# An output product with standing weights: six of eight chunk pairs turned, their sums transposed in 32x32 blocks behind the next pair

## The chip, the cores and the metric

The kernel runs on one core of a Trainium2 chip. The metric is the device time of one execution in microseconds (us). Before the change it is 1220.3 us, the median of three runs (1218.64 to 1220.49).

## The reference

What is computed, in NumPy, cut to what matters (4608 tokens of 512 features go in the middle part, all in float32):

```
a  = softmax(scale * x @ state.T);   xread = a @ state
a2 = softmax(scale * state @ x.T);   sread = a2 @ x
x  = concatenate([xread, sread], axis=2)        # (8, 8, 544, 64)
x  = x.transpose(0, 2, 1, 3).reshape(4352, 512)
h  = maximum(x @ w_in, 0)                       # 512 -> 2048
y  = h * h @ w_out                              # 2048 -> 512
h  = (y @ w1) * (y @ w2) @ w3                   # 512 -> 1024 -> 1024
out = h @ w_out2                                # (4352, 512)
```

The change concerns the last two lines, and there the product with `w3 @ w_out2`, which the kernel forms once as one matrix.

## The kernel before

The tokens are cut in eight chunks (one per batch) of 512 read tokens; the 256 state tokens of all batches are a ninth, small chunk. After the attention and the first feed-forward network, whose result `y` lies in DRAM, about 711 us into the span, the second network begins. It goes over the chunks in **two sweeps** (s=0 and 1, one for each half of the 1024 hidden features), each over four **pairs** of chunks, `turns = [(3,4), (5,6), (7,2), (0,1)]` forward and then backward. A pair of chunks is taken together because both feature products and output products are done by a fast matrix scheme for 2x2 blocks with seven block products instead of eight; the sums and differences of blocks that it needs are made on VectorE (DVE). Every float32 operand is split in a high and a low part (`split`: a cast on ScalarE, ACT, then a subtraction on DVE, L81 and L82), and each block product runs three passes (HI*HI, LO*HI, HI*LO).

A pair consists of four `quad` calls (L941, m = 0 to 3), seven products of six matmuls with 512 columns each (L945), and then an **out stage**, `out_pair` (L1071). In a quad, `kept` copies a bank from PSUM on ACT (L953, tiles `s0` to `s3`), `plus` adds another bank on DVE (L957), the two multiplications at L975 and L981 give `q1` and `q0`, and `to_z` (L901) makes from them the blocks B11, T1 and so on, that the out stage reads (tiles `z`, slots `c1` to `c6`). What is not needed at once is split later, by `late_z` (L923) inside the out stage.

`out_pair` runs seven products A11*B11, S1*T1, S4*B22, A12*B21, S2*T2, S3*T3 and A22*T4 (L1090). In each, a 128x128 block of **tokens stands** in PE and 256 columns of **weights move**: 24 matmuls per product. `keep` (L1111) copies a bank to SBUF on ACT, `put` (L1123) adds the other bank on DVE and stores the sum of output block "11", "12", "21" or "22" (two tiles each): in the first sweep by a plain DMA on the SP queue, in the second by an accumulating DMA on the POOL queue (L1136). Pair (3,4), the first of sweep 0 and the last of sweep 1, is the exception: its sums wait in a DRAM scratch (`oscr`), and in its last stage (`ends`) they are fetched and added before the only store. The tiles of the blocks are named by `AT`: block "11" lies in the slots `s0` and `s1`, which the next quad's `kept` uses too.

`load_turn` (L1059) replaces one of the four weight slots in the course of the stage (with the combinations for S4, then for S3), on the SP queue. `jobs` are pieces of the next pair's preparation (`make_pair`, splits of `yraw` into `yq`), put between the products. The order of the instructions on an engine follows from the written order and from a scheduler that fills in; `issue_after` keeps a piece behind a named instruction. Each engine works through its own list in order: an instruction that waits holds up what stands behind it.

Of the kernel before, what the change touches and what calls it, by code (L numbers as in the profile page):

```python
# [20 lines left out]
def kernel(  # L21
# [17 lines left out]
    nc = tc.nc  # L39
# [255 lines left out]
    def att_steps(b):  # L295
# [5 lines left out]
        def xpose(k):  # L301
            ps = bank_m("ps_x") if b else bank_y(k, "ps_x")
            for j in range(J):
                h0 = 2 * (k % 2)
                nc.tensor.transpose(
                    ps[:, j * P:(j + 1) * P],
                    X[b, k // 2][:, j, h0:h0 + 2, :].rearrange("p h d -> p (h d)"), ident,
                )
            t = att.tile([P, 512], F32, tag="xT", bufs=4, name="xT")
            xT[b, k] = t  # L310
            if b == 0 and k == HG - 1:
                return nc.vector.tensor_copy(t, ps)
            return nc.scalar.copy(t, ps)

        def scores():
            pss = [bank_m("ps_s") for _ in range(G)]
# [71 lines left out]
        def a2_T(r):  # L388
            ps = bank_m("ps_a2")
            e = v["a2", r]  # L390
            for j in range(J):
                nc.tensor.transpose(ps[:, j * P:(j + 1) * P], e[:, j * P:(j + 1) * P], ident)
            nc.scalar.copy(e, ps)

        def sread():
# [502 lines left out]
    def minus(t, a, b):  # L898
        return nc.vector.tensor_tensor(out=t, in0=a, in1=b, op=ALU.subtract)  # L899

    def to_z(m, q0, q1):  # L901

        idx = m // 2
        if m % 2 == 0:
            z_split(1 + idx, "B11", idx, q0)
            minus(q0, q1, q0)
            left["T1", idx], left["B12", idx] = q0, q1
            return z_split(3 + idx, "T1", idx, q0)
# [12 lines left out]
        return last  # L921
# [16 lines left out]
            z_split(6, "T4", 0, left.pop(("T4", 0)))  # L938
            z_split(2, "T4", 1, left.pop(("T4", 1)))

    def quad(c0, c1, m):  # L941
        def product(ps, w, v, first=True, last=True):
            for kt in range(2):
                for k, (wi, vi) in enumerate(PASSES):
                    nc.tensor.matmul(  # L945
                        ps, W[w, kt][:, wi, m * P:(m + 1) * P], Y[v, kt][:, vi, :],
                        start=(first and kt == 0 and k == 0), stop=(last and kt == 1 and k == 2),
                        skip_group_check=True,
                    )

        def kept(i, ps):
            t = bp.tile([P, 512], F32, tag=f"s{i}", bufs=1 + (i == 0), name=f"s{i}")
            left["copy"] = nc.scalar.copy(t, ps)  # L953
            return t

        def plus(t, ps):
            nc.vector.tensor_tensor(out=t, in0=ps, in1=t, op=ALU.add)  # L957
# [7 lines left out]
        plus(p1, E)  # L965
# [3 lines left out]
        plus(u2, D)  # L969
        product(C, "A22", "T4")  # L970
        product(A, "S3", "T3", first=False)
        u3 = kept(3, A)
        plus(p5, A)
        q1 = bp.tile([P, 512], F32, tag="qd" if m % 2 else "qb", bufs=1 if m % 2 else 2, name="q1")
        nc.vector.tensor_tensor(out=q1, in0=u2, in1=p5, op=ALU.mult)  # L975
        plus(u3, C)
# [4 lines left out]
        nc.vector.tensor_tensor(out=q0, in0=p1, in1=u3, op=ALU.mult)  # L981
        return to_z(m, q0, q1)

    def load9(pool, tag):
        ts = []
# [81 lines left out]
    def place(tag, name):  # L1067
        pool = pa if tag in ("yo", "r") else bp
        return pool.tile([P, 512], F32, tag=tag, bufs=2 if tag in TWO else 1, name=name)

    def out_pair(c0, c1, s, jobs, last, first, more):  # L1071
        ends = s == 1 and not more
        jobs, gate = list(jobs), left["copy"]
# [49 lines left out]
        def put(block, ts, ps, tp0=0):  # L1123
            c, i = where(block)
            for tp, t in enumerate(ts, tp0):
                nc.vector.tensor_tensor(out=t, in0=ps[tp - tp0], in1=t, op=ALU.add)  # L1126
                if s == 0 and first:
                    nc.sync.dma_start(scr(c, i, tp), t)
                    continue
                rows_t = "(p j) e -> p j e" if c < BLK else "(j p) e -> p j e"  # L1130
# [43 lines left out]
            load_turn(s, 1)  # L1174
        if ends:
            bC = [bank_y((2 + t) % 4, "oc") for t in range(4)]
            rows_t = "(p j) e -> p j e" if c0 < BLK else "(j p) e -> p j e"
# [38 lines left out]
    bp = ctx.enter_context(tc.tile_pool(name="bp", bufs=1, reuse_waits="tile"))  # L1216

    turns = [(3, 4), (5, 6), (7, 2), (0, 1)]
    raw9 = load9(bp, "s0")
    raw = load_pair(*turns[0])  # L1220
    make9(raw9)
# [4 lines left out]
    for s, todo in enumerate((turns, turns[::-1])):  # L1226
        if s == 1:
            for t in range(NT9 // P):
                load_o9(t)
        for m in range(QM):  # L1230
            ab9(m)
        for t in range(NT9 // P):
            out9(t, s)
        load_sums(s)
        load_turn(s, 1)
        for i, (c0, c1) in enumerate(todo):
            for m in range(QM):
                last = quad(c0, c1, m)
# [12 lines left out]
            out_pair(c0, c1, s, jobs, last, i == 0, more)  # L1251
# [33 lines left out]
```

## Time and profile before

| | |
|---|---|
| runs | 1218.64, 1220.3, 1220.49 us |
| profiled execution | 1219.03 us, span 1217.3 us |
| granted clock | 0.999 |
| busy in the span: PE / PE weight loads / DVE / ACT / POOL | 1201.4 / 999.6 / 869.4 / 662.2 / 109.4 us |
| a pair of the second sweep | 58.27 us: four quads of 9.5 us and an out stage of 20.2 us |

The profile is one execution, 1.7 us longer than its span. The chain that ended last is followed backward from the end; PE makes up most of it, which means that a stretch of time is as long as PE's work in it, unless PE waits. Busy time of another engine matters where PE, or a store at the end, waits for it.

### The profile page before, as it was taken

Reading aid. Unit: us, or ns where it says so; the run is one execution under the profiler, and the core shown is the slowest. Engines: PE = TensorE matmul, PEld = TensorE weight load, DVE = VectorE, ACT = ScalarE, POOL = GpSimd, SP = SyncE. Lnnn points to the kernel's source line nnn. Section 1 sums busy time; section 2 is a strip of 40 time slices with the busy share of each in tenths; the row PEclk is TensorE's granted clock in tenths of the full one; section 3 lists DMA queues with packets and bytes.
Section 4 is the critical chain, followed back from the end, with each engine's and each line's share of the span. In section 5 each row is a group of like instructions: output and inputs, shape, how many; then the busy total and the mean of one; then the engine's idle time right before and its main releaser. Section 6 shows DMA issues by size and latency. Waiting matters only on the chain.

```text
span 1217.3 us, 18891 instructions
## 1 busy us (share of the span) xinstructions
PE 1201.4 (99%) x7174; PEld 999.6 (82%) x7174; DVE 869.4 (71%) x1594; ACT 662.2 (54%) x1220; POOL 109.4 (9%) x163
## 2 busy tenths in 40 slices
PE   7999999999999999999999999999999999999998
PEld 5677777777778777778899888989898989898988
DVE  6968877677586766742435875878696957877877
ACT  6877466555464655654656653546363635453542
POOL 0000001322421121100000000000000000211110
PEclk9999999999999999999999999999999999999999
DMA  9445664835446397630413642223232540716244
GB/s 260 138 140 173 159 184 145 185 113 130 129 127 156 106 184 155 154 53 35 121 53 113 222 156 98 81 93 104 70 104 70 191 138 20 155 30 144 49 74 138
DMA packets 147922, 150.66 MB, mean 124 GB/s; under 512 B 81016, under 2 KB 107128, under 8 KB 147320
## 3 DMA queue, kind: packets, MB, share of 16 engines
q1 hardware_dynamic: 120968, 106.20, 29.6%
q0 software_dynamic: 26576, 43.00, 15.6%
q8 instruction: 56, 0.92, 0.3%
q14 instruction: 34, 0.28, 0.1%
q10 hardware_dynamic: 288, 0.26, 0.1%
HBM read 99.61 MB, written 55.05 MB: 127 GB/s over the span
## 4 chain that ended last, share of the span: by engine, by line
PE 89%; DMA 4%; DVE 3%; ACT 3%; SPq 1%; issue 0%; DVEq 0%; ACTq 0%
PE y L524 29%; PE qa L945 11%; PE qd L945 7%; PE oa L1096 5%; PE od L1096 4%; PE qc L945 4%; PE qe L945 4%; PE ps_sw L454 2%; PE ab L1006 2%; PE oe L1096 2%; PE oc L1096 2%; DMA yraw<-yscr 1%; DMA raw<-in_moe_w_in_dram 1%; PE po L1036 1%; PE ps_r L400 1%; PE ps_s L320 1%
## 5 line engine op out<-in xcount | busy, mean ns | idle before, releaser
L524 PE MATMUL y<-ghl,wo 128*128 128x512 f32 (+1 forms) x1728 | 398.9, 380 | 0.5 <-ACT ghl L81 0.5
L524 PEld LDWEIGHTS y<-ghl,wo 128*128 128x128 f32 x1728 | 310.3, 188 | 74.9 <-issue 13.4
L82 DVE TENSOR_TENSOR ghl<-r,ghl 128x512 fp32r<-128x512 f32 (+1 forms) x144 | 95.1, 660 | 163.2 <-ACT ghl L81 138.7
L953 ACT COPY s<-qa 128x512 f32<-128x512 f32 x96 | 56.5, 589 | 180.1 <-PE qa L945 179.3
L945 PE MATMUL qa<-yq,wq 128*128 128x512 f32 x576 | 143.7, 389 | 0.0
L945 PEld LDWEIGHTS qa<-yq,wq 128*128 128x128 f32 x576 | 107.7, 188 | 22.0
L945 PE MATMUL qd<-yq,wq 128*128 128x512 f32 x384 | 97.4, 389 | 0.0
L82 DVE TENSOR_TENSOR z<-q,z 128x512 fp32r<-128x512 f32 x112 | 74.3, 687 | 23.7 <-ACT z L81 23.6
L473 ACT ACTIVATE r<-r 128x512 f32<-128x512 f32 (+1 forms) x144 | 87.7, 609 | 3.2
L81 ACT CAST ghl<-r 128x512 fp32r<-128x512 f32 (+1 forms) x144 | 86.0, 597 | 3.6
L945 PEld LDWEIGHTS qd<-yq,wq 128*128 128x128 f32 x384 | 72.1, 188 | 15.0
L1136 POOL DMA_DIRECT2D out_dram<-o x24 | 28.6, 1597 | 598.2 <-DVE o L1126 598.0
L81 ACT CAST z<-q 128x512 fp32r<-128x512 f32 x112 | 68.1, 625 | 20.2 <-PE oe L1096 7.4
L957 DVE TENSOR_TENSOR s<-qa,s 128x512 f32<-128x512 f32 x32 | 22.1, 692 | 69.8 <-ACT s L953 69.8
L82 DVE TENSOR_TENSOR yq<-yraw,yq 128x512 fp32r<-128x512 f32 x98 | 64.6, 686 | 4.2 <-ACT yq L81 4.2
L81 ACT CAST yq<-yraw 128x512 fp32r<-128x512 f32 x98 | 59.3, 625 | 12.5 <-DVE yraw L874 7.6
L945 PE MATMUL qe<-yq,wq 128*128 128x512 f32 x192 | 48.7, 389 | 0.0
L945 PE MATMUL qc<-yq,wq 128*128 128x512 f32 x192 | 48.7, 389 | 0.0
L770 PE MATMUL ps_w<-wo,w3T 128*128 128x512 f32 x192 | 44.0, 390 | 0.3 <-ACT u L81 0.3
L899 DVE TENSOR_TENSOR q<-q,q 128x512 f32<-128x512 f32 x64 | 43.1, 684 | 0.0
L770 PEld LDWEIGHTS ps_w<-wo,w3T 128*128 128x128 f32 x192 | 35.9, 188 | 8.1 <-ACT u L81 0.7
L945 PEld LDWEIGHTS qc<-yq,wq 128*128 128x128 f32 x192 | 36.0, 188 | 7.5
(598 smaller groups left out, 2059.5 us busy)
## 6 DMA issues: line engine op xcount, KB each, us to landing
yraw<-yscr SPq DMA_DIRECT2D x56, 256.0 KB, 5.4
yscr<-yo SPq DMA_DIRECT2D x52, 256.0 KB, 3.1
raw<-in_moe_w_out_dram SPq DMA_DIRECT2D x16, 512.0 KB, 4.3
raw<-in_moe_w_dram POOLq DMA_DIRECT2D x64, 128.0 KB, 3.5
raw<-in_moe_w_dram POOLq DMA_DIRECT2D x16, 512.0 KB, 5.0
raw<-in_moe_w_in_dram SPq DMA_DIRECT2D x12, 512.0 KB, 4.2
out_dram<-o SPq DMA_DIRECT2D x24, 256.0 KB, 2.7
out_dram<-o POOLq DMA_DIRECT2D x24, 256.0 KB, 6.6
```

Of the source, the lines that this page charges most:

```text
L81: nc.scalar.copy(hi, src)
L82: return nc.vector.tensor_tensor(out=lo, in0=src, in1=f32(hi), op=ALU.subtract)
L454: mm = nc.tensor.matmul(pss[r][k * NS:(k + 1) * NS, cols], stT[rows, b, k, :], win_t[fg][rows, k, cols], start=True, stop=True, tile_posit ...
L473: nc.scalar.activation(r[:, :n], r[:, :n], ACTF.Square)
L524: nc.tensor.matmul(y_ps[c, d][:, :n], wo_t[f][:, wi, d * P:(d + 1) * P], t[:, gi, :n], start=(f == f0 and k == 0), stop=(f == f1 - 1 and k ...
L770: nc.tensor.matmul(ps, t[:, wi, (j % 4) * P:(j % 4 + 1) * P], wo2_t[j][:, vi, :], start=(j == 0 and k == 0), stop=(j == N1 - 1 and k == 2),)
L899: return nc.vector.tensor_tensor(out=t, in0=a, in1=b, op=ALU.subtract)
L945: nc.tensor.matmul(ps, W[w, kt][:, wi, m * P:(m + 1) * P], Y[v, kt][:, vi, :], start=(first and kt == 0 and k == 0), stop=(last and kt == ...
L953: left["copy"] = nc.scalar.copy(t, ps)
L1006: nc.tensor.matmul(pss[i][:, :NT9], w[:, wi, m * P:(m + 1) * P], Y[B, d][:, vi, :NT9], start=(d == 0 and k == 0), stop=(d == ND - 1 and k ...
L1096: nc.tensor.matmul(ps[tp][:, t % 2 * NH:(t % 2 + 1) * NH], Z[v, idx][:, vi, t * P:(t + 1) * P], rhs[:, wi], start=(first and t % 2 == 0 an ...
L1136: nc.gpsimd.dma_start(dst, src, accum_op=ALU.add)
```

## The change

Six of the eight out stages, all but those of pair (3,4), are done by a new `turned_pair`: a 128x128 block of the **weights stands**, and all 512 **tokens** of a chunk **move**: 12 matmuls with 512 columns per product instead of 24 with 256. The result has features in partitions and tokens in columns, so it can't be stored to the output as it is. It is stored to the scratch `oscr` as whole tiles of 256 KB, by plain DMAs on SP in sweep 0 and by accumulating DMAs on POOL in sweep 1. In sweep 1 each tile is fetched again during the next pair (`drain_load`, SP, 8 tiles for a pair), transposed in 32x32 blocks on DVE (`drain_store`), and stored to the output in four DMAs, two on SP and two on POOL, each of 512 runs of 128 bytes. The output tiles of the transposes rotate over three buffers (`to` and two of `yo`). To make the tokens of all chunks come in plain order, batch 0 and its like are loaded and turned with another stride at the start of the kernel.

The product A22*T4 accumulates in the bank of A11, S2 and S3, with one more copy of block "21" on ACT and one DVE add fewer for each tile. The splits of B11 and T1 for m=2 (`even_z(1)`) move from quad m=2 to quad m=3: to its beginning where nothing is drained, behind its last product where the pair drains (pairs two, three and four of sweep 1).

```diff
@@ load_xj @@
-            nc.sync.dma_start(t[:, j], x[b, g * HG:(g + 1) * HG, j::J].rearrange("h p d -> p h d"))
+            nc.sync.dma_start(t[:, j], x[b, g * HG:(g + 1) * HG, j * P:(j + 1) * P].rearrange("h p d -> p h d"))
...
-            if b == 0 and k == HG - 1:
-                return nc.vector.tensor_copy(t, ps)
-            return nc.scalar.copy(t, ps)
+            if b:
+                return nc.scalar.copy(t, ps)
+            t, ps = t.rearrange("q (p j) -> q j p", j=J), ps.rearrange("q (j p) -> q j p", j=J)
+            return (nc.vector.tensor_copy if k == HG - 1 else nc.scalar.copy)(t, ps)
...
+    def even_z(idx):
+        q0, q1 = left["T1", idx], left["B12", idx]
+        z_split(1 + idx, "B11", idx, q0)
+        minus(q0, q1, q0)
+        return z_split(3 + idx, "T1", idx, q0)
...
+    def drain_load(slot):
+        t = bp.tile([P, 2, 512], F32, tag=f"c{slot}", bufs=1, name="tr")
+        for n in range(2):
+            key = drains.pop(0)
+            nc.sync.dma_start(t[:, n], scr(*key))
+            taken.append((key, t[:, n]))
+
+    def drain_store():
+        (c, i, e), t = taken.pop(0)
+        pool, tag, bufs = (bp, "to", 1) if len(taken) % 3 == 0 else (pa, "yo", 2)
+        o = pool.tile([P, 512], F32, tag=tag, bufs=bufs, name="to")
+        nc.vector.transpose(out=o, in_=t)
+        e0 = i * NH + e * P
+        for a in range(P // NS):
+            cols, rows = slice(e0 + a * NS, e0 + (a + 1) * NS), slice(a * NS, (a + 1) * NS)
+            (nc.gpsimd if a % 2 else nc.sync).dma_start(
+                out[c * T:c * T + S, cols].rearrange("(b i) e -> i b e", i=NS),
+                o[rows].rearrange("i (b e) -> i b e", e=NS),
+            )
...
+    def turned_pair(c0, c1, s, jobs, last, more):
...
+        def product(ps, w, v, first=True, last=True):
+            for e in range(2):
+                cols = slice(e * P, (e + 1) * P)
+                for idx in range(NB):
+                    lhs = block(w, s * NB + idx, idx)
+                    for k, (wi, vi) in enumerate(PASSES):
+                        nc.tensor.matmul(
+                            ps[e], lhs[:, wi, cols], Z[v, idx][:, vi, :],
+                            start=(first and idx == 0 and k == 0), stop=(last and idx == NB - 1 and k == 2),
...
+                if s == 0:
+                    nc.sync.dma_start(scr(*key), t)
+                else:
+                    nc.gpsimd.dma_start(scr(*key), t, accum_op=ALU.add)
+                    drains.append(key)
...
+        t21 = keep("21", bA)
+        put("22", t22, t21)
+        if more:
+            load_turn(s, 1)
+        product(bA, "A22", "T4", first=False)
+        put("21", keep("21", bA, t21))
...
+            steps = [[], [], [], [lambda: even_z(1)] if not drains else []]
+            if drains:
+                put, get = drain_store, drain_load
+                steps[1] = [put, nothing, lambda: (put(), get(2))]
+                steps[2] = [put, lambda: (put(), get(4)), put, put]
+                steps[3] = [put, put, lambda: even_z(1)]
...
+            if (c0, c1) == turns[0]:
+                out_pair(c0, c1, s, jobs, last, i == 0, more)
+            else:
+                turned_pair(c0, c1, s, jobs, last, more)
```

The change moves instructions; three places are shown. The first is **DVE at the end of the last quad and in the out stage of pair three of sweep 1**. `s` are a quad's sums, `q` its products, `z` the blocks for the out stage (the low parts), `to<-tr` is a transpose. Before, from the quad's last drains on:

```order
L957 TENSOR_TENSOR s_11232<-qa,s_11232 128x512
L957 TENSOR_TENSOR s_11268<-qc,s_11268 128x512
L975 TENSOR_TENSOR q_11271<-s_11247,s_11232 128x512
L981 TENSOR_TENSOR q_11274<-s_11224,s_11268 128x512
L899 TENSOR_TENSOR q_11205<-q_11271,q_11205 128x512
L899 TENSOR_TENSOR q_11202<-q_11271,q_11202 128x512
L82 TENSOR_TENSOR z<-q_11271,z 128x512
L82 TENSOR_TENSOR z<-q_11274,z 128x512
```

and with the change:

```order
L969 TENSOR_TENSOR s_10927<-qa,s_10927 128x512
L82 TENSOR_TENSOR z<-q_10907,z 128x512
L987 TENSOR_TENSOR q_10985<-s_10948,s_10927 128x512
L1095 STREAM_TRANSPOSE to<-tr 128x512
L902 TENSOR_TENSOR q_10907<-q_10898,q_10907 128x512
L969 TENSOR_TENSOR s_10975<-qc,s_10975 128x512
L902 TENSOR_TENSOR q_10898<-q_10985,q_10898 128x512
L82 TENSOR_TENSOR z<-q_10907,z 128x512
L993 TENSOR_TENSOR q_10988<-s_10919,s_10975 128x512
L902 TENSOR_TENSOR q_10907<-q_10985,q_10907 128x512
L82 TENSOR_TENSOR z<-q_10985,z 128x512
L82 TENSOR_TENSOR z<-q_10988,z 128x512
```

Twelve operations stand where eight stood: a transpose and three of `even_z(1)` are new here. Behind them both lists go on alike for 13 operations, up to the two adds `o<-oe,o` that complete block "11".

The second is **ACT at the start of the quad behind that stage** (pair two; pair three is alike). `o<-oa` are copies of the stage, `s` those of the quad, from bank `qa` (A) and `qd` (D); what an instruction waits for stands in brackets, DMASW being stores issued on POOL. Before:

```order
L1119 COPY o<-oa 128x512 [waits DMASW4_49,PE_49,Activation_49]
L953 COPY s_11005<-qa 128x512 [waits PE_49]
L953 COPY s_11013<-qd 128x512 [waits DMASW6_49,PE_49]
L81 CAST yq<-yraw 128x512 [waits DVE_49] x3
L953 COPY s_11028<-qa 128x512 [waits PE_49]
```

and with the change:

```order
L81 CAST yq<-yraw 128x512 [waits DVE_49] x2
L965 COPY s_10667<-qd 128x512 [waits DMASW6_49,PE_49]
L965 COPY s_10659<-qa 128x512 [waits PE_49]
L1137 COPY o<-oa 128x512 [waits DVE_49,Activation_49] x2
L965 COPY s_10682<-qa 128x512 [waits PE_49]
```

The copy of D, which waits for a POOL store, now stands ahead of the copy of A.

The third is **PE at the end of the kernel**, in the last stage. `oa<-w34b` is S3*T3, whose weights `load_turn` brings, `od<-w34b` S4*B22, `oa<-s` S2*T2 and `oc` A22*T4. Before:

```order
L1096 MATMUL oa<-s_9847,z 128x256 x3
L1096 MATMUL oa<-s_9850,z 128x256 x3
L1189 MATMUL oc<-w34b,z 128x256 x9
L1096 MATMUL oa<-w34b,z 128x256 x24
L1189 MATMUL oc<-w34b,z 128x256 x15
```

and with the change:

```order
L1208 MATMUL od<-w34b,z 128x256 x24
L1208 MATMUL oa<-s_9613,z 128x256 x3
L1208 MATMUL oa<-s_9616,z 128x256 x3
L1301 MATMUL oc<-w34b,z 128x256 x12
L1208 MATMUL oa<-w34b,z 128x256 x24
```

S3*T3 now comes last, and nearer behind S4*B22 (`od<-w34b`, 24 matmuls), which before ended 41 matmuls ahead of it.

## Rows read from the trace of the kernel before

**Rows 1.** The page: busy time by engine, and the chain that ended last.
```profile
PE 1201.4 (99%) x7174; PEld 999.6 (82%) x7174; DVE 869.4 (71%) x1594; ACT 662.2 (54%) x1220; POOL 109.4 (9%) x163
...
PE 89%; DMA 4%; DVE 3%; ACT 3%; SPq 1%; issue 0%; DVEq 0%; ACTq 0%
```

**Rows 2.** Chain: start us, us, what; an out stage of sweep 0, then a quad.
```profile
826.51 2.87 PE oa L1096 x24
...
873.89 2.72 PE qa L945 x12
```

**Rows 3.** One pair by stretches: PE, PEld, DVE, ACT, POOL busy; PEclk, DMA share, GB/s.
```profile
1038.40:1048.00 9.60, 9.60 (x44) 7.94 (x43) 8.90 (x15) 4.22 (x7) 5.56 (x5) 1.00 1.19 188
1048.00:1057.50 9.50, 9.50 (x43) 7.86 (x43) 5.68 (x9) 3.39 (x6) 0.00 (x0) 1.00 0.77 238
...
1080.00:1085.00 5.00, 5.00 (x44) 5.00 (x43) 5.00 (x9) 4.77 (x10) 0.00 (x0) 1.00 0.00 0
1085.00:1090.00 5.00, 5.00 (x44) 5.00 (x43) 5.00 (x10) 3.33 (x7) 0.00 (x0) 1.00 0.32 105
1090.00:1096.67 6.67, 6.67 (x57) 6.67 (x57) 6.67 (x12) 2.98 (x6) 3.97 (x4) 1.00 0.69 78
```

**Rows 4.** Groups by form, 780 to 1217 us: busy us, mean ns, idle before.
```profile
L945 PE MATMUL qa<-yq,wq 128*128 128x512 f32 x504 | 126.0, 389 | 0.0
...
L81 ACT CAST yq<-yraw 128x512 fp32r<-128x512 f32 x76 | 46.1, 625 | 4.2 <-DVE yraw L874 3.5
```

**Rows 5.** Timeline of DVE in an out stage of sweep 1: start us, us, what.
```profile
1018.94 0.69 DVE L957 TENSOR_TENSOR s<-qa,s 128x512 f32<-128x512 f32 x1 [2.27 <-ACT s L953]
1019.55 0.68 DVE L957 TENSOR_TENSOR s<-qc,s 128x512 f32<-128x512 f32 x1
...
1031.60 1.28 DVE L1126 TENSOR_TENSOR o<-oe,o 128x512 f32<-128x512 f32 x2
```

**Rows 6.** Timeline of ACT in an out stage of sweep 0.
```profile
828.07 0.59 ACT L1119 COPY o<-oa 128x512 f32<-128x512 f32 x1
828.55 1.15 ACT L81 CAST yq<-yraw 128x512 fp32r<-128x512 f32 x2
```

**Rows 7.** POOL's timeline in the stage of rows 5; landing of those two.
```profile
1032.58 2.44 POOL L1136 DMA_DIRECT2D out_dram<-o  x2 [498.29 <-DVE o L1126]
...
DMA to landing us min/median/max: 4.0/5.6/7.1
```

**Rows 8.** Timeline of ACT in the quad behind that stage.
```profile
1039.86 0.59 ACT L953 COPY s<-qa 128x512 f32<-128x512 f32 x1 [3.44 <-PE qa L945]
1041.22 0.59 ACT L953 COPY s<-qd 128x512 f32<-128x512 f32 x1 [0.77 <-PE qd L945]
```

**Rows 9.** The last stage: PE's timeline, DVE's last row, landing of the turn loads (L1061).
```profile
1203.57 1.36 PE L1096 MATMUL oe<-w34b,z 128*128 128x256 f32 x10
...
1208.49 3.04 PE L1096 MATMUL oa<-w34b,z 128*128 128x256 f32 x24
1211.37 1.96 PE L1189 MATMUL oc<-w34b,z 128*128 128x256 f32 x15
...
1212.78 1.41 DVE L1183 TENSOR_TENSOR opart<-oc,opart 128x256 f32<-128x256 f32 x4
...
DMA to landing us min/median/max: 2.6/3.3/5.6
```

**Rows 10.** A transpose by form; the SP queue, 140 to 150 us: packets, MB, share.
```profile
L279 DVE STREAM_TRANSPOSE xT<-xb 128x512 f32<-128x512 f32 x20 | 13.5, 693 | 0.0
...
q1 hardware_dynamic: 4368, 1.05, 51.2%
```

**Rows 11.** Issues on POOL by form: busy us, mean ns.
```profile
L214 POOL DMA_DIRECT2D raw<-in_moe_w_dram x64 | 34.4, 545 | 33.8 <-DVE cw L152 24.3 <-DVE x9T L413 3.8 <-DVE xT L279 3.6
...
L229 POOL DMA_DIRECT2D yscr<-yscr x5 | 9.6, 1911 | 1.4 <-issue 1.2
```

**Rows 12.** Waits of PE, 0 to 60 us: total, times, longest.
```profile
PE ps_sw L454 <- ACT xT L313: 2.1, 2, 1.8
```

More of the change, by code (lines that the diff above doesn't have):

```diff
@@ L391, in a2_T @@
             for j in range(J):
-                nc.tensor.transpose(ps[:, j * P:(j + 1) * P], e[:, j * P:(j + 1) * P], ident)
+                nc.tensor.transpose(
+                    ps[:, j * P:(j + 1) * P], e[:, j * P:(j + 1) * P] if b else e[:, j::J], ident,
+                )
             nc.scalar.copy(e, ps)
@@ L899, in minus, with to_z @@
         return nc.vector.tensor_tensor(out=t, in0=a, in1=b, op=ALU.subtract)
-    def to_z(m, q0, q1):
+    def even_z(idx):
[3 more added lines that the diff above has]
+        return z_split(3 + idx, "T1", idx, q0)
+    def to_z(m, q0, q1, q_last):
         idx = m // 2
         if m % 2 == 0:
-            z_split(1 + idx, "B11", idx, q0)
-            minus(q0, q1, q0)
             left["T1", idx], left["B12", idx] = q0, q1
-            return z_split(3 + idx, "T1", idx, q0)
+            return even_z(idx) if m == 0 else q_last
         t1, b12 = left.pop(("T1", idx)), left.pop(("B12", idx))
@@ L939, in late_z, with behind_jobs, quad @@
             z_split(2, "T4", 1, left.pop(("T4", 1)))
-    def quad(c0, c1, m):
+    def behind_jobs(gate, jobs):
+        with tc.issue_after(gate.ins):
+            for job in jobs:
+                job()
+    def quad(c0, c1, m, mids=()):
         def product(ps, w, v, first=True, last=True):
@@ L956, in plus @@
         def plus(t, ps):
-            nc.vector.tensor_tensor(out=t, in0=ps, in1=t, op=ALU.add)
+            return nc.vector.tensor_tensor(out=t, in0=ps, in1=t, op=ALU.add)
         A, D, E, C = bank_m("qa"), bank_y(m % 2, "qd"), bank_y(2, "qe"), bank_y(3, "qc")
@@ L964, in quad @@
         product(E, "A12", "B21")
-        plus(p1, E)
+        behind_jobs(plus(p1, E), mids[:1])
         product(A, "S2", "T2", first=False, last=False)
@@ L968, in quad @@
         product(D, "S4", "B22", first=False)
-        plus(u2, D)
+        behind_jobs(plus(u2, D), mids[1:2])
         product(C, "A22", "T4")
@@ L972, in quad @@
         u3 = kept(3, A)
-        plus(p5, A)
+        behind_jobs(plus(p5, A), mids[2:3])
         q1 = bp.tile([P, 512], F32, tag="qd" if m % 2 else "qb", bufs=1 if m % 2 else 2, name="q1")
         nc.vector.tensor_tensor(out=q1, in0=u2, in1=p5, op=ALU.mult)
-        plus(u3, C)
+        behind_jobs(plus(u3, C), mids[3:])
         if m % 2:
@@ L980, in quad @@
             q0 = pa.tile([P, 512], F32, tag="r", bufs=2, name="q0")
-        nc.vector.tensor_tensor(out=q0, in0=p1, in1=u3, op=ALU.mult)
-        return to_z(m, q0, q1)
+        return to_z(m, q0, q1, nc.vector.tensor_tensor(out=q0, in0=p1, in1=u3, op=ALU.mult))
     def load9(pool, tag):
@@ new lines, in turned_pair, with do, late, block @@
+    def turned_pair(c0, c1, s, jobs, last, more):
+        jobs, gate = list(jobs), left["copy"]
+        def do(n):
+            with tc.issue_after(last.ins), tc.issue_after(gate.ins):
+                for job in jobs[:n]:
+                    job()
+            del jobs[:n]
+        def late(n):
+            with tc.issue_after(last.ins):
+                late_z(n)
+        def block(w, u, idx):
+            if w in ("S1", "S2"):
+                return S12[idx][:, int(w == "S2")]
+            return w34_t[u][:, {"A11": 0, "A12": 2, "A22": 3}.get(w, 1)]
+        def product(ps, w, v, first=True, last=True):
[7 more added lines that the diff above has]
+                            start=(first and idx == 0 and k == 0), stop=(last and idx == NB - 1 and k == 2),
+                            skip_group_check=True,
+                        )
+        def keep(name, ps, ts=None):
+            ts = ts or [place(AT[name][e], "o") for e in range(2)]
+            for t, p in zip(ts, ps):
+                nc.scalar.copy(t, p)
+            return ts
+        def put(name, ts, ps=None):
+            k, i = OUTS[name]
+            for e, t in enumerate(ts):
+                if ps:
+                    nc.vector.tensor_tensor(out=t, in0=ps[e], in1=t, op=ALU.add)
+                key = ((c0, c1)[k], i, e)
+                if s == 0:
[3 more added lines that the diff above has]
+                    drains.append(key)
+        bA = [bank_h("oa") for _ in range(2)]
+        product(bA, "A11", "B11", last=False)
+        t11 = keep("11", bA)
+        late(0)
+        bD = [bank_m("od") for _ in range(2)]
+        product(bD, "S1", "T1", last=False)
+        t22 = keep("22", bD)
+        do(2)
+        late(1)
+        product(bD, "S4", "B22", first=False)
+        load_turn(s, 2)
+        late(2)
+        do(1)
+        bE = [bank_y(d, "oe") for d in range(2)]
+        product(bE, "A12", "B21")
+        put("11", t11, bE)
+        late(3)
+        do(1)
+        product(bA, "S2", "T2", first=False, last=False)
+        t12 = keep("12", bA)
+        put("12", t12, bD)
+        do(1)
+        product(bA, "S3", "T3", first=False, last=False)
+        t21 = keep("21", bA)
[4 more added lines that the diff above has]
+        put("21", keep("21", bA, t21))
+        do(len(jobs))
@@ L1218 @@
     turns = [(3, 4), (5, 6), (7, 2), (0, 1)]
+    taken = []
+    nothing = lambda: None
     raw9 = load9(bp, "s0")
@@ L1236 @@
         for i, (c0, c1) in enumerate(todo):
+            steps = [[], [], [], [lambda: even_z(1)] if not drains else []]
[4 more added lines that the diff above has]
+                steps[3] = [put, put, lambda: even_z(1)]
             for m in range(QM):
-                last = quad(c0, c1, m)
+                last = quad(c0, c1, m, steps[m])
+                if m == 0 and drains:
+                    drain_load(2)
+                    drain_load(4)
                 if m == 0 and i + 1 < len(todo):
```

7 lines of the change are left out of this document (4 added, 3 removed).

## The prediction, made before the changed kernel was run

> **What bounds the kernel now.** I read the page first. PE is busy for 1201.4 of 1217.3 us and makes up 89% of the chain that ended last [rows 1], so a step counts by what it does to PE's stream: matmuls that get cheaper, or waits that open between them. The chain cut to one out stage shows 24 matmuls of 256 columns in 2.87 us, and elsewhere 12 of 512 columns in 2.72 us, with nothing between [rows 2]. The table by stretches, over one pair of the second sweep, shows who has room: DVE is busy all of the out stage (5.00 of 5.00) and 8.90 of 9.60 us in quad m=0; the DMA engines are loaded in the first two quads and at the stage's end [rows 3]. Forms and timelines give prices: a 512-column matmul takes 389 ns from start to end and steps every 227 ns, a cast on ACT 625 ns [rows 4]; DVE starts 512-column operations 0.60 us apart [rows 5]; ACT starts the next operation 0.48 us behind a copy [rows 6].
>
> **The products.** Six of the eight out stages turn: 6 x 7 = 42 products of 12 x 226.7 ns (2.72 us) instead of 24 x 120.0 ns (2.88 us). 42 x 0.16 = **-6.72 us**, if PE stays fed. Both steps are columns over 2.4 GHz plus 13.3 ns, so the gain is 13.3 ns for each of the 504 matmuls dropped. In the Trainium skill, "TensorE: Matmul & The Clock Gate", section "Back-to-back issue gap", the isolated gap is 2.5 ns over that: 109.2 and 215.8 ns, hence only 0.03 us for each product, an estimate of 1.3 us in all. The trace has both forms at 120.0 and 226.7 ns, and the measurement decides.
>
> **Costs that are hidden.** Copies on ACT: two more for each turned stage (block 21 is copied twice), 12 x 0.59 us, where ACT is at 3.33 of 5.00 us in the second part of the stage [rows 3]; two DVE adds fewer. The 24 transposes cost DVE 0.60 us each (one of that size took 693 ns, as an add does [rows 10]), 8 for each of three pairs, in quads m=1 to m=3 and the stage's start; quad m=1 has 5.68 of 9.50 us busy [rows 3], so by throughput they fit. The start writes batch 0's transposes with a stride; PE waited 2.1 us for those copies [rows 12]. From nothing to 0.6 us more or less; I take nothing. The first turned stages (three of the first sweep, one of the second) keep the plain order, and each half's copy has the other half's six matmuls (1.36 us) of cover.
>
> **Pairs two and three of the second sweep** (stages that drain). First, S2T2's two halves end one matmul after the other, and S3T3 goes into the same bank: the matmul's 0.39 and the copy's 0.59 us less two steps of 0.23 leave 0.5 to 0.6 us; I take 0.6, twice: **+1.2 us**.
>
> Second, a wait behind a store. DVE's queue from the quad's last drain to the add of block 11 grows from 21 operations to 25 (the last transpose and three of the moved `even_z`). Before, that queue ran from 1018.94 to 1031.60 without a hole [rows 5], so the add comes 4 x 0.60 = 2.4 us later. Its two POOL accumulates were issued 14.46 and 15.68 us into the stage, which began at 1018.12; the second landed 7.1 us after issue [rows 7]. Now the second is issued 15.7 + 2.4 = 18.1 us into a stage of 84 x 0.2267 = 19.04 us, plus the 0.6 and eight matmuls of the next pair that PE's order pulls forward (1.81): 21.45. The next quad's copy of D goes into that tile (`s1`), and ACT's new order has it *ahead of* the copy of A that S2T2 waits for; before, A's came first (1039.86, then 1041.22 [rows 8]). S2T2 is due after ten more matmuls (2.27), at 23.7. With landing L, ACT's two copies (1.1) end at 18.1 + L + 1.1, so the stall is L - 4.5. Ends: L = 4.0, the first of a pair [rows 7], gives nothing; 7.4, since the copy at 1041.22 did not wait [rows 8], gives 2.9. The pieces are now 2 KB instead of 1 KB and fewer accumulates follow, but the turn load still falls beside it: I take 6.0, hence 1.5 us, twice: **+3.0 us** (0 to 5.8).
>
> **The last stage** keeps 256-column products, but its feed moves. `even_z(1)` now comes after quad m=3's last product, behind a transpose. The replay by hand from the stage's start: PE gets through 36 matmuls (4.32 us) before T1,1. ACT can begin that slot's first cast only when PE has read the slot for the last time, at about 3.9 us; two casts (0.52 + 0.62) put T1,1's HI part at 5.05: wait 0.73. Its LO part is one DVE operation (0.68) behind, with two matmuls between: 0.47. B22,1 waits 0.24 in the same way, and T4, cast when its slot is free, 0.45 for HI and 0.47 for LO. Together 2.4 us. S3T3 then ends the kernel, and its weights are a turn load that may start only after S4B22's last use of the slot. Before, 41 matmuls lay between, 1203.57 to 1208.49 [rows 9]; now about 20, 2.3 us of cover against a landing of 2.6 to 5.6, median 3.3 [rows 9]: 1.0 (0.4 to 3.3). **+3.4 us**.
>
> The **tail**: before, DVE ended at 1214.19, 0.86 us after PE's 1213.33 [rows 9], since only half adds were left. Now two full adds (0.60 each) and four half adds (1.41 together [rows 9]) stand behind the last matmul, 0.86 + 1.9 us: **+1.9 us**.
>
> **Sum:** -6.72 + 1.2 + 3.0 + 3.4 + 1.9 = +2.8 us on the profiled execution's 1219.03 us (span 1217.3 and 1.7 around it): **1221.8 us**. That execution is 1.3 us under the runs' median of 1220.3 and 0.4 above their fastest. A measurement of this kernel can tell about 0.2%, 2.4 us, from no change, so my forecast stands just over that edge: the gain on PE is eaten by waits of the same size.
>
> **Rivals.**
> *The accumulates land early.* If the second one of a pair takes 4.5 us or less, the wait in pairs two and three is gone: 1218.8 us, no change. For: the first of a pair took 4.0 [rows 7], and pieces are twice as long. Against: the second took 7.1. If the last stage's waits were hidden as well (ACT or DVE some 0.7 us earlier than in my replay, at each place), 3.4 us more go: 1215.4, faster.
>
> *The stores clog the DMA engines.* 96 stores move 512 runs of 128 bytes each. The nearest rows are reads: eight loads of 64 KB in such runs, with a 512 KB load, took at most 51.2% of 10 us [rows 10], so at most 0.64 us each. A pair has 24.9 us of DMA before (shares by lengths [rows 3]); 32 stores add at most 20.5, and 8 loads of 256 KB about 8: 53 of 58 us, just enough. From some 0.75 us for a store the engines are full; at 0.9 they need 4 us more for each of the two pairs that also load a next one: 1221.8 + 8 = 1230 us. DVE would wait for a free buffer at the third or fourth transpose, and PE behind it. For it speaks that no row shows a write of short runs. The Trainium skill, "DMA: Bandwidth & Descriptors", section "Specifications", speaks for it too: below 512 bytes a transfer is done as read-modify-write; no run here shows that.
>
> *POOL's queue.* 16 stores of a pair are issued there. Rows bound one between 0.55 us (128 KB) and 1.9 us (1 MB in 512-byte runs) [rows 11]. Above some 1.6 us the eight transposes of two and a half quads (24 us) wait for POOL; at 1.9 that is 16 x 0.3 = 5 us for each of two pairs: 1232 us. I take 0.8, hidden.
>
> *The turned products bring nothing like 6.72 us*, because PE steps the new 512-column stream (weights of one product in 12 blocks) slower than the quads' 226.7 ns. By the skill's gap it would be 1227; no row speaks for it.
>
> **How the numbers follow.** Forecast 0.40 (from 1219 to 1224.6 by the bounds of L; half of it more than 2.4 us above before). Early landing 0.22 (no change), with a hidden last stage too 0.15 (faster). Stores 0.13, POOL 0.05, slow products 0.05 (all slower). Faster: 0.15 + 0.05 from the edge of the early case = 0.20. Slower: 0.20 + 0.23 = 0.43. Same: 0.37. The range takes in the hidden last stage at its lower end and the stores at 0.9 us at its upper: 1215 to 1229.5.
>
> **What would show it.** Right: products of 2.72 us in the turned stages; PE idle some 1.5 us early in the quad behind the stages of pairs two and three, put down to an ACT copy that itself waited for a POOL store; five short waits and one for a weight load in the last stage; DVE ending about 2.8 us after PE. Wrong: transposes that wait for stores, POOL rows of over 1.6 us for a drain store, DMA share near 1.00 through all four quads, or no waits behind the turned stages at all.

## The result, and the profile after

The changed kernel takes **1228.51 us**, the median of six runs (1225.82 to 1231.82), against 1219.91 for the kernel before (six runs, 1217.48 to 1220.49): 1.0077 times as long, 95% interval 1.0058 to 1.0096. The forecast was 1221.8 (1215 to 1229.5): the time lies inside the range, near its upper end. The profiled execution took 1228.43 us with a span of 1226.6, so 9.3 us more in the span than before. One run in the whole record stands far apart, 3626.64 us for the kernel `no_drain` below, and the figures there leave it out.

The page of the changed kernel, busy time and chain by engine (against [rows 1]):

```profile
PE 1202.0 (98%) x6670; PEld 974.4 (79%) x6670; DVE 877.7 (72%) x1606; ACT 668.7 (55%) x1232; POOL 132.6 (11%) x211
...
PE 85%; DMA 5%; DVE 4%; issue 3%; ACT 2%; SPq 1%; POOL 0%; DVEq 0%; ACTq 0%; POOLq 0%
```

504 matmuls are gone, yet PE is busy for 0.6 us longer, and its idle time grew from 15.9 to 24.6 us (span less busy time). Its share of the chain fell by four points. Where, the stages tell. Their starts, from the first matmul of each quad and stage in PE's timeline, give this budget of the span:

| stretch | before, us | after, us | difference |
|---|---|---|---|
| start of the span to the first turned stage's beginning | 826.35 | 828.07 | +1.72 |
| four turned stages without drains | 20.16 each | 19.15 each | -4.0 |
| two turned stages with drains | 20.16 each | 20.02 | -0.3 |
| the ninth chunk and the quads behind it | 55.10 | 55.22 | +0.1 |
| quads behind the two draining stages | 38.10 each | 40.21, 42.34 | +6.35 |
| last stage to the end | 24.4 | 29.8 | +5.4 |

(Eight matmuls of a quad that PE's order pulls ahead into the draining stages, 1.81 us, are counted with their quad. The other quads took 38.1 us in both.)

The chain through the first turned stage (start us, us, what; against [rows 2]):

```profile
1017.07 2.72 PE oa L1128 x12
1019.79 5.55 PE od L1128 x24
1025.34 2.72 PE oe L1128 x12
1028.06 8.16 PE oa L1128 x36
```

Six of the seven products take the 2.72 us that the forecast used, twelve steps of 226.7 ns. One takes 2.83 (5.55 - 2.72), for which the trace names no wait. The stage is 19.15 long instead of 19.04.

All waits of PE from 770 us to the end (before, this view was empty):

```profile
PE qa L957 <- ACT s L965: 4.1, 2, 2.5
PE oa L1128 <- ACT o L1137: 0.9, 2, 0.4
PE od L1208 <- ACT z L81: 0.7, 1, 0.7
PE oc L1301 <- ACT z L81: 0.4, 1, 0.4
PE oa L1208 <- DMA w34b<-w34u: 0.3, 1, 0.3
PE oc L1301 <- DVE z L82: 0.2, 1, 0.2
PE od L1208 <- DVE z L82: 0.2, 1, 0.2
```

Every place that the prediction named is in it, but for B22's cast. The first row is the quads' sums, and there lies the largest difference. POOL's timeline at the end of the first draining stage (against [rows 7]):

```profile
1091.20 1.82 POOL L1149 DMA_DIRECT2D oscr<-o  x2 [12.05 <-DVE o L1144]
```

And the view of that line, from issue to landing of these two:

```profile
DMA to landing us min/median/max: 5.2/6.2/7.1
```

The chain there:

```profile
1091.80 7.10 DMA oscr<-o
...
1100.11 1.66 PE qa L957 x6
```

And ACT's timeline (against [rows 8]):

```profile
1098.98 0.59 ACT L965 COPY s<-qd 128x512 f32<-128x512 f32 x1 [4.42 <-DMA oscr<-o]
1099.46 0.59 ACT L965 COPY s<-qa 128x512 f32<-128x512 f32 x1
```

The copy of D (`qd`) stood on ACT for 4.42 us until the accumulate had landed, and the copy of A (`qa`) stood behind it, although A's product had ended at about 1097.57 (six matmuls from 1096.05 on, 1.52 us together, in PE's timeline). PE then starts S2T2 at 1100.11. Behind the second draining stage the chain has the same piece with 8.02 us of landing:

```profile
1151.99 8.02 DMA oscr<-o
```

PE's timeline shows what the two waits cost; read it from start to start, since the idle time in brackets counts only from the modelled end of the last matmul:

```profile
1097.41 1.07 PE L957 MATMUL qe<-yq,wq 128*128 128x512 f32 x4
1100.11 1.66 PE L957 MATMUL qa<-yq,wq 128*128 128x512 f32 x6 [1.62 <-ACT s L965]
1101.60 1.54 PE L957 MATMUL qd<-yq,wq 128*128 128x512 f32 x6
...
1157.63 1.07 PE L957 MATMUL qe<-yq,wq 128*128 128x512 f32 x4
1161.21 2.92 PE L957 MATMUL qa<-yq,wq 128*128 128x512 f32 x6 [2.51 <-ACT s L965]
1163.93 1.66 PE L957 MATMUL qd<-yq,wq 128*128 128x512 f32 x6
```

Four steps after 1097.41, at 1098.32, the next matmul was due: 1.79 us late. After 1157.63 it is 2.67. And the six matmuls behind the second wait step from 1161.21 to 1163.93, 0.453 us each, twice the usual 0.227. The table by stretches says why (length, busy time of PE, PEld, DVE, ACT and POOL with counts, PEclk, DMA share, GB/s):

```profile
1155.00:1160.00 5.00, 3.70 (x17) 2.73 (x15) 5.00 (x9) 0.00 (x0) 3.09 (x4) 1.00 1.09 228
1160.00:1162.00 2.00, 0.79 (x2) 0.70 (x3) 0.70 (x2) 1.92 (x4) 0.37 (x2) 0.68 1.13 207
1162.00:1166.00 4.00, 4.00 (x15) 2.97 (x13) 0.69 (x2) 1.97 (x5) 1.67 (x2) 0.73 1.06 227
```

The granted clock is a mix of its two levels, 2.4 and 1.2 GHz, over these two stretches: TensorE ran at the lower one for part of them, after it had stood still for 2.5 us.

The last stage in PE's timeline (against [rows 9]):

```profile
1200.98 0.40 PE L1208 MATMUL oe<-w34b,z 128*128 128x256 f32 x2
1202.05 0.50 PE L1208 MATMUL od<-s,z 128*128 128x256 f32 x2 [0.68 <-ACT z L81]
1202.78 2.17 PE L1208 MATMUL od<-s,z 128*128 128x256 f32 x16 [0.22 <-DVE z L82]
1204.79 2.57 PE L1208 MATMUL oe<-w34b,z 128*128 128x256 f32 x18
1207.72 0.50 PE L1301 MATMUL oc<-w34b,z 128*128 128x256 f32 x2 [0.35 <-ACT z L81]
1208.44 1.46 PE L1301 MATMUL oc<-w34b,z 128*128 128x256 f32 x10 [0.23 <-DVE z L82]
...
1215.49 1.60 PE L1301 MATMUL oc<-w34b,z 128*128 128x256 f32 x12
1217.43 3.34 PE L1208 MATMUL oa<-w34b,z 128*128 128x256 f32 x24 [0.34 <-DMA w34b<-w34u]
```

DVE's timeline ends with:

```profile
1222.14 1.41 DVE L1295 TENSOR_TENSOR opart<-oc,opart 128x256 f32<-128x256 f32 x4
```

From start to start, with 0.12 us for a matmul, T1 is late by 0.83 (HI) and 0.49 (LO), T4 by 0.77 and 0.48, the turn load by 0.50. PE ends at 1220.77 and DVE at 1223.55, 2.78 behind it.

### The profile page after: what moved, and what is told of

It reads as the page before. It is cut to its first block, busy times and chain, and to the rows that moved or that the text cites. A ratio compares the mean times of both kernels' runs of the same rounds, so it can differ in the third digit from the quotient of the medians.

```text
span 1226.6 us, 18148 instructions
## 1 busy us (share of the span) xinstructions
PE 1202.0 (98%) x6670; PEld 974.4 (79%) x6670; DVE 877.7 (72%) x1606; ACT 668.7 (55%) x1232; POOL 132.6 (11%) x211
## 4 chain that ended last, share of the span: by engine, by line
PE 85%; DMA 5%; DVE 4%; issue 3%; ACT 2%; SPq 1%; POOL 0%; DVEq 0%; ACTq 0%; POOLq 0%
PE y L527 29%; PE qa L957 10%; PE qd L957 7%; PE qc L957 4%; PE oa L1128 4%; PE qe L957 3%; PE ps_sw L457 2%; PE ab L1017 2%; PE od L1128 2%; PE oa L1208 1%; DMA oscr<-o 1%; DMA yraw<-yscr 1%; PE od L1208 1%; PE po L1047 1%; PE oe L1128 1%
## 5 line engine op out<-in xcount | busy, mean ns | idle before, releaser
L957 PEld LDWEIGHTS qd<-yq,wq 128*128 128x128 f32 x384 | 72.3, 188 | 15.2
L1149 POOL DMA_DIRECT2D oscr<-o x24 | 20.9, 989 | 532.8 <-DVE o L1144 530.5
L81 ACT CAST yq<-yraw 128x512 fp32r<-128x512 f32 x98 | 57.2, 627 | 12.4 <-DVE yraw L877 7.0
```

Source lines behind the costliest of these rows:

```text
L81: nc.scalar.copy(hi, src)
L957: nc.tensor.matmul(ps, W[w, kt][:, wi, m * P:(m + 1) * P], Y[v, kt][:, vi, :], start=(first and kt == 0 and k == 0), stop=(last and kt == ...
```

## The experiments

Five of them change one part of the changed kernel (in `own_tr` and `last_wide` the buffers of the fetched tiles and, with them, the place of `even_z(1)`); `start_only` is the kernel before with one part of the change; the last four try another order. Each ratio is to the kernel before, run on the same chip.

**Is the start slower?** `start_only` is the kernel before with the new token order alone (the strided loads, transposes and copies of the start, and plain rows at the output).

```diff
-            nc.sync.dma_start(t[:, j], x[b, g * HG:(g + 1) * HG, j::J].rearrange("h p d -> p h d"))
+            nc.sync.dma_start(t[:, j], x[b, g * HG:(g + 1) * HG, j * P:(j + 1) * P].rearrange("h p d -> p h d"))
...
-                rows_t = "(p j) e -> p j e" if c < BLK else "(j p) e -> p j e"
+                rows_t = "(j p) e -> p j e"
```

> The kernel before with only the new token order of the chunks 0 to 2 (loads of x, strided copies of batch 0, the stores' pattern); no turned stage. Theory: the strided copies are late for PE and open holes in which PE's granted clock falls to half for longer, so the first quad starts 1.6 us later and the whole is 1 to 2 us slower than before. Rival: the later start in the changed kernel's profile is chance of one execution: within 0.5 us of before.

Measured: 1219.59 us, 1.0002 (0.9993 to 1.0011): the rival came true. The start costs nothing that can be measured, at most 1.3 us. The 1.7 us of the profiled execution are at least in part chance of one execution: in the eleven profiles of this study that have the new start, the first pair's quads go on behind the ninth chunk's products at 732.9 (`early`) to 734.5 us (the changed kernel), 733.7 in the mean, with 732.73 in the one profile of the kernel before. All eleven are later than that one, so a start that costs some tenths of a us isn't ruled out.

**Is it the buffer?** `s2_buf` puts the second tile of block "11" into the slot `s2`, which the next quad needs later than `s1`.

```diff
         def keep(name, ps, ts=None):
+            if name == "11":
+                ts = [place("s0", "o"), place("s2", "o")]
```

> The changed kernel, but the second tile of output block 11 lies in the slot s2 instead of s1, which the next quad writes one product and a half later. Theory: the two waits of PE on an ACT copy behind a POOL store (2.1 and 2.5 us, and about 1.7 us of half clock after the second) shrink to under 1 us together: 4 to 6 us less than the changed kernel. Rival: the store's landing moves the wait to the next copy and little is gained: under 1.5 us less.

Measured: 1221.90 us, 1.0020 (1.0011 to 1.0029), 6.6 us less than the changed kernel; the quads behind the draining stages lost 6.35 in the budget. PE's waits of `s2_buf` from 770 us on begin so, and the rest of the view has no `qa` either:

```profile
PE oa L1210 <- DMA w34b<-w34u: 1.4, 1, 1.4
PE oa L1128 <- ACT o L1139: 0.9, 2, 0.4
PE od L1210 <- ACT z L81: 0.7, 1, 0.7
```

PE's order in the two draining stages is the same, and on ACT the copy of D still stands ahead of that of A (1092.53, then 1096.61), but it no longer waits for a store. The stretches of quads behind those stages take 38.36 and 38.39 us, so 5.8 of the 6.35 us are gone; the wait for the turn load in the last stage grew instead. That settles this term: the wait, and the half clock behind it, come from the one tile that two owners share.

**What do the drains cost as a whole?** `no_drain` leaves out the fetching, the transposes and the 96 stores.

```diff
                     nc.gpsimd.dma_start(scr(*key), t, accum_op=ALU.add)
-                    drains.append(key)
+                    pass
```

> The changed kernel with all drains left out: no fetch, no transpose, no store of six chunks' output, and the splits of B11 and T1 for m=2 early in quad m=3 in every pair. Theory: the products themselves bring 1.0 us in each of six stages and nothing waits, so about 6 us less than the kernel before (ratio 0.995), with a last stage as long as before (24.4 us). Rival (the turned stages cost PE something of their own, or the start does): at most 3 us less than before.

Measured: 1214.52 us (the median of five runs), 0.9961 (0.9948 to 0.9974). PE waits for nothing from 770 us on, all six turned stages are 19.15 us long and the last stage takes 24.4, as before the change. So the products' own gain is 4.8 us (3.2 to 6.3) by the runs; six stages that are 1.01 shorter make 6.1, and in its profile a start 0.9 us later than in the profile before takes a part of that back. By the two ratios (1.0077 - 0.9961), the drains cost the changed kernel 14 us.

**Is it the stores?** `few_stores` keeps one block of each transposed tile.

```diff
-        for a in range(P // NS):
...
+        for a in range(1):
+            nc.sync.dma_start(out[c * T:c * T + NS, e0:e0 + NS], o[:NS, :NS])
```

> The changed kernel without the 96 stores of 128-byte runs (one 32x32 block per transposed tile is stored, so most of the output of six chunks' pairs is left out); loads and transposes stay. Theory: the stores are hidden, so at most 1 us less than the changed kernel. Rival (the stores clog the DMA engines or POOL): the waits behind the turned stages and in the last stage go, 4 to 8 us less.

Measured: 1223.07 us, 1.0026 (1.0015 to 1.0037), 5.4 less than the changed kernel, where at most 1 was expected. It does not tell what it was meant to tell: with fewer stores the scheduler gave PE another order (72 instead of 58 matmuls of the draining stages stand in one piece), the copy's waits shrank from 4.1 to 3.3 us, no half clock followed them, and the last stage took 26.3 instead of 29.8. Order and stores are mixed.

**Is it the place of `even_z(1)`?** `own_tr` fetches the tiles into other buffers (those of the split products, `ghl`), so that `even_z(1)` can go back to quad m=2.

```diff
-            return even_z(idx) if m == 0 else q_last
+            return even_z(idx)
...
-        t = bp.tile([P, 2, 512], F32, tag=f"c{slot}", bufs=1, name="tr")
+        t = pa.tile([P, 2, 512], F32, tag="ghl", bufs=3, name="tr")
```

> The changed kernel, but the fetched tiles lie in buffers of their own, so that the splits of B11 and T1 for m=2 stand in quad m=2 again, as before the change; drains, transposes and stores stay. Theory: the last stage loses its waits of 0.7 and 0.2 us for B11 and T1 and some of the rest (1 to 2.5 us less), and the add of block 11 in the stages of pairs two and three comes 1.8 us earlier, which shortens the waits behind the POOL stores by up to 1.8 us each: 3 to 6 us less than the changed kernel. Rival: only the last stage gains, 1 to 2 us.

Measured: 1252.32 us, 1.0267 (1.0253 to 1.0281): a miss. Those buffers are also the next pair's `yq`, so the fetches waited for PE's last reads of it. The first transpose of a pair began at 1070.06 instead of 1051.5, and the rest fell into the out stage. DVE's timeline of `own_tr`:

```profile
1070.06 0.71 DVE L1095 STREAM_TRANSPOSE to<-tr 128x512 f32<-128x512 f32 x1 [0.34 <-DMA tr<-oscr]
```

And the first rows of PE's waits in it, from 770 us on:

```profile
PE oa L1208 <- DVE opart L1228: 10.4, 1, 10.4
PE od L1128 <- ACT o L1137: 7.0, 4, 2.3
PE oa L1128 <- DVE z L82: 3.2, 4, 1.3
```

It says nothing on `even_z(1)`, but gives a price: drains that slip behind the quads cost some 24 us more. In the out stage DVE has no room [rows 3].

**The last pair's tiles elsewhere.** `last_wide` fetches them into the idle weight buffers `wi1`, transposes in m=1 and m=2, and does `even_z(1)` at the start of m=3, for that pair alone.

```diff
+            wide = bool(drains) and i + 1 == len(todo)
+            if wide:
+                steps = [[], [put, put, put], [put, put, put, put], [lambda: even_z(1), put]]
...
+                if m == 0 and wide:
+                    drain_wide()
```

> The changed kernel, but in the last pair the eight tiles are fetched into the two raw buffers that no next pair needs, transposed in quads m=1 and m=2, and the splits of B11 and T1 for m=2 come early in quad m=3. Theory: the last stage loses its waits and most of its tail, 24.5 to 27 us instead of 29.8, so 3 to 5 us less than the changed kernel; the waits behind the stages of pairs two and three stay. Rival: it is the store traffic at the end that holds the last stage: under 1 us less.

Measured: 1225.33 us, 1.0047 (1.0035 to 1.0059), 3.2 less than the changed kernel. The waits for T1 and T4 (2.57 us) are gone, but the last stage takes 28.0 us instead of 29.8, not the 24.5 to 27 expected, because the next wait grew: the chain through its last stage now has a turn load that landed late.

```profile
1207.79 2.89 PE od L1216 x24
...
1210.77 4.96 DMA w34b<-w34u
1215.73 0.14 issue
1215.86 3.65 PE oa L1216 x18
```

**The drains earlier.** `early` moves the drains' steps half a quad forward, so that all eight transposes are done when quad m=3 starts, and puts `even_z(1)` behind m=3's first product.

```diff
-                steps[1] = [put, nothing, lambda: (put(), get(2))]
-                steps[2] = [put, lambda: (put(), get(4)), put, put]
-                steps[3] = [put, put, lambda: even_z(1)]
+                steps[1] = [put, lambda: (put(), get(2)), put, lambda: (put(), get(4))]
+                steps[2] = [put, put, put, put]
+                steps[3] = [lambda: even_z(1)]
```

> The changed kernel with the drains placed half a quad earlier (four transposes in m=1, four in m=2), so that the splits of B11 and T1 for m=2 come early in quad m=3 in all three pairs that drain; buffers as in the change. Theory: DVE's queue in the stages of pairs two and three is as short as before the change, the accumulates are issued some 2 us earlier and the copies behind them wait little, and the last stage loses its waits: 7 to 10 us less than the changed kernel. Rival: the fetched tiles are not there so early, DVE waits for them and PE with it: 3 us less or none, or slower than the changed kernel.

Measured: 1217.09 us, 0.9976 (0.9967 to 0.9984), 11.4 us less than the changed kernel; run once more as `early_again` on another chip, 1216.67 us, 0.9980 (0.9971 to 0.9988).

> The variant with the drains half a quad earlier once more, on the same chip as the one with small stores, to compare the two: about 0.998 of the kernel before, as before.

The same work in another order is faster than the kernel before. All six turned stages take 19.15 us, and the quads 38.1. The accumulates land no sooner (4.0 and 7.7 us), but the first is issued at 1087.08, 14.5 us into its stage instead of 17.0, and ACT's timeline has A ahead of D again:

```profile
1093.34 0.59 ACT L965 COPY s<-qa 128x512 f32<-128x512 f32 x1 [2.46 <-PE qa L957]
...
1095.47 0.59 ACT L965 COPY s<-qd 128x512 f32<-128x512 f32 x1 [0.69 <-DMA oscr<-o]
```

D still waits for the store, 0.69 us, and PE no longer waits for D. What is left stands in the last stage, 27.0 us against 24.4 before: -6.1 + 2.6 = -3.5 us by the stages, -2.9 by the ratio of the runs.

**All remedies at once.** `early2_s2_wide` joins the edits of `s2_buf` and `last_wide` with an order close to that of `early`:

```diff
+                steps[1] = [put, lambda: (put(), get(2)), put, lambda: (put(), get(4))]
+                steps[2] = [nothing, put, put, put]
+                steps[3] = [lambda: (put(), even_z(1))]
```

> All remedies together: block 11's second tile in s2, the last pair's tiles in the raw buffers, the drains of the other pairs half a quad earlier (the last one at the start of m=3). Theory: most of the products' 6 us is left: 2 to 5 us less than the kernel before. Rival: some wait takes the place of those removed: no better than the kernel before.

Measured: 1216.09 us, 0.9976 (0.9966 to 0.9986): no better than `early`. Its last stage takes 26.8 us; T4's wait is gone and the turn load's took its place (1.5 us in all).

**The stores once more.** `early_thin` is `early` with 32 instead of 512 runs in each store.

```diff
-                out[c * T:c * T + S, cols].rearrange("(b i) e -> i b e", i=NS),
-                o[rows].rearrange("i (b e) -> i b e", e=NS),
+                out[c * T:c * T + NS, cols], o[rows, :NS],
```

> The variant with the drains half a quad earlier, each of its 96 stores moving one 32x32 block (32 runs of 128 bytes) instead of sixteen, so that 15/16 of the drained output is left out; the order on the engines is nearly that of the variant, in contrast to the changed kernel without stores, where the scheduler gave another one. Theory: the short runs are hidden, within 1.5 us of the variant with full stores. Rival: the stores load the DMA engines so that other transfers land late: 3 to 5 us less than that variant.

Measured: 1213.78 us, 0.9954 (0.9940 to 0.9967), 2.9 less than `early_again`, beside which it ran: more than the 1.5 expected, and just under the rival's 3. The gain lies in the last stage alone, 24.9 against 27.0 us; from the first quad to there both take 454.1 to 454.3 us, as `no_drain` does. But PE's order in the last stage is another one too (A12*B21 is cut in pieces, and S4*B22 comes ahead of T4's product), so whether the stores or the order take those 2 us stays open. What the stores take of the DMA engines can be read, in the table by stretches, over the quads and the out stage of one pair. `early_again`:

```profile
1034.96:1092.37 57.41, 57.41 (x254) 47.15 (x252) 50.49 (x83) 29.73 (x54) 17.35 (x24) 1.00 0.73 169
```

`early_thin`:

```profile
1035.70:1092.91 57.21, 57.21 (x253) 47.22 (x252) 50.33 (x83) 29.82 (x54) 14.93 (x24) 1.00 0.51 133
```

`no_drain`:

```profile
1035.24:1092.48 57.24, 57.24 (x254) 47.22 (x252) 45.48 (x75) 29.66 (x54) 6.87 (x8) 1.00 0.40 91
```

(0.73 - 0.51) x 57.3 = 12.6 us for 15/16 of 32 stores, 0.42 us each; (0.51 - 0.40) x 57.2 less the thin stores' share leaves 5.5 us for eight fetches.

## Why the prediction was right, and where it was off

The direction, the places and the mechanisms were right; the copy of D was sized far too small, and what the half clock costs was not in the sum.

That the time lies in the range is partly luck. For its own mechanisms the forecast gave 1219 to 1224.6 us, and 1228.5 is beyond that. The range reached to 1229.5 because it took in a rival, the stores at 0.9 us each, and that rival didn't happen.

| term | forecast, us | profile after, us |
|---|---|---|
| products | -6.72 | -6.1 |
| S3T3 behind the copy, two stages | +1.2 | +1.7 |
| copy of D behind the accumulate, two quads | +3.0 | +6.35 |
| last stage on PE | +3.4 | +3.5 |
| tail on DVE | +1.9 | +1.9 |
| start and the rest | 0 | +1.9 |
| sum | +2.8 | +9.3 |

- **Products**: 2.72 us as priced, with one product of 2.83 in each stage: 19.15 for 19.04. The rival that PE would step the new stream more slowly is out. So is the estimate by the isolated gap of the Trainium skill's "TensorE: Matmul & The Clock Gate", section "Back-to-back issue gap": the new stream steps 226.7 ns (2.72/12) as the quads do, not 215.8.
- **S3T3**: S2T2's last two matmuls start at 1088.06 and S3T3 at 1089.13 in PE's timeline; less two steps that is 0.62, as forecast. The other 0.25 of a stage is lost in small pieces where products alternate.
- **The copy of D**: this is the term that was off, by 3.35 us. 1.46 of them lie in the waits: from start to start PE lost 1.79 and 2.67 us instead of 1.5 each. The other 1.9 was not in the prediction at all: matmuls behind the waits that ran slower, 1.36 + 0.14 us of it at the half clock behind the second. `s2_buf` removes 5.8 of the whole 6.35.
- **The landing in that term**, "I take 6.0", was a choice between two rows and stood for neither. In the three stages of the second sweep before, the view of L1136 has 7.1, 7.4 and 7.5 us for the second accumulate of the first pair; in the two draining stages after it was 7.10 and 8.02. Pieces of 2 KB instead of 1 KB made the issue shorter (two in 1.82 us against 2.44 [rows 7]), not the landing. Nor did the drain stores make it longer: in `no_drain` it is 7.7 and 7.3 in the same two stages.
- **Two errors the other way** hid part of that. By the prediction's L - 4.5 the landings of 7.10 and 8.02 would have cost 2.6 and 3.5 us. But the second accumulate's issue began 17.58 us into the stage, not 18.1: the prediction put the second issue before at 15.68, half of the 2.44 us behind the first, and it began at 1033.3, which is 15.2 (start of both in the view of that line below). The delay of 2.4 us on DVE was as forecast. And S2T2 was due at 24.1, not 23.7.

```profile
L1136 POOL DMA_DIRECT2D out_dram<-o x2: 1227/1458/1689, 1032.6 to 1033.3; - x2
```

- **The last stage**: 2.57 us in four waits for casts against 2.4 in five, and 0.50 for the turn load against 1.0. Errors cancelled, which is luck: B22 did not wait, T1 and T4 waited somewhat longer, and 0.30 that was not foreseen lies inside S3T3 (3.34 us against 3.04 before). `last_wide` shows that the turn load is what comes next once the casts are early.
- **The tail**: 2.78 us behind PE, as forecast.
- **The start**: nothing that the runs can tell, as taken; `start_only` leaves at most 1.3 us. The 1.9 in the table is that of the two profiled executions.
- **The accumulates land early** is out (7.10 and 8.02 against the 4.5 it needed). **The stores clog the DMA engines** is out for all but the last stage: 0.42 us for a store, under the 0.64 of the bound and far from 0.9, and no transpose waited for a buffer. (The prediction called the engines full at a share of 1.00; [rows 3] has 1.19, so that was no limit.) By the Trainium skill's "DMA: Bandwidth & Descriptors", "Specifications", runs of 128 bytes would be read, changed and written; no row here shows whether they are. **POOL's queue** is out: a drain store holds POOL for 0.65 us, 0.8 was taken.

The prediction treated the terms as separate prices. The order shows their common root: the drains stood so late that their last transposes and `even_z(1)` were queued on DVE ahead of everything the out stage needed. `early` moves them and the three terms of waits shrink together, to a kernel that is faster than the one before by 0.2%.

## What to carry to other kernels

Follow a late operation through the buffers, not only through its engine: an operation more on DVE delayed a store, the store held a tile, the tile held a copy on ACT, and the copy held another on which PE waited. If two accumulating stores follow each other, price the second by the second one's landing, as the trace before has it. When a background job costs more than its work, first move it earlier; where its order comes from a scheduler, compare the order again after each edit, since fewer or smaller stores changed the matmuls' order here in `few_stores` and `early_thin`.

## What was not expected of the hardware

- After PE had stood still for 2.5 us the granted clock fell: six matmuls took 2.72 us instead of 1.36. After the wait of 1.6 us at 1098.5 six took 1.49, and the table by stretches shows 1.00 up to the second wait. The length of the wait alone doesn't decide it: in `last_wide`, whose waits at the same two places are 2.1 and 2.6 us, the clock fell behind the first (six matmuls in 2.56 us) and not behind the second (six in 1.49). Its table by stretches, behind each wait:

```profile
1100.00:1104.00 4.00, 3.77 (x10) 2.96 (x11) 0.12 (x1) 2.14 (x5) 1.72 (x2) 0.57 1.08 194
1162.00:1166.00 4.00, 3.15 (x13) 2.48 (x14) 0.59 (x2) 3.24 (x7) 1.72 (x2) 1.00 1.03 146
```

- In the first 100 us the mean granted clock differs between profiles with the same start: 0.91 in `start_only`, 0.95 after and 0.98 in `early` (0.98 before, with the other start). The row of `start_only` in the table by stretches:

```profile
0.00:100.00 100.00, 90.41 (x620) 64.78 (x620) 75.43 (x160) 70.97 (x132) 0.69 (x6) 0.91 0.55 166
```

- A pair of accumulating stores of 256 KB lands unevenly, with the same bytes: 4.0 and 7.1 us after their issues before, 5.2 and 8.0 at the second place after, 4.0 and 7.7 in `early`, 4.2 and 7.7 in `no_drain`. No run here shows why.
